# Packed attention and a two-layer network on one core: small-tile products in runs over four PSUM banks, a last chunk of 128 keys, a new order

## Chip, core and metric

The kernel runs on one core of a Trainium2 chip. The metric is the device time of one execution in microseconds (us); several runs are taken and their median counts. The profile is one execution, recorded by the hardware profiler.

## What is computed

For 8 batches of 576 tokens with 8 heads of 64, 32 packed queries a head attend to the keys and values, and the tokens then attend to the 32 packed results. What comes out goes through two layers, 512 to 2048 to 512, with an ELU between them.

```python
def sm_attn(qq, kk, vv):
    s = scale * np.matmul(qq, kk.transpose(0, 1, 3, 2))
    s = s - np.max(s, axis=-1, keepdims=True)
    a = np.exp(s)
    a = a / (np.sum(a, axis=-1, keepdims=True) + 1e-09)
    return np.matmul(a, vv)
p_packed = sm_attn(p, k, v)
out = sm_attn(q, p_packed, p_packed)
...
h = x @ w_in
g = np.where(h > 0.0, h, alpha * (np.exp(np.minimum(h, 0.0)) - 1.0))
return (g @ w_out).astype(np.float32)
```

All arrays are float32, 8 x 8 x 576 x 64 for q, k and v, 8 x 8 x 32 x 64 for p, 512 x 2048 and 2048 x 512 for the weights.

## The kernel before

**Attention of a batch** (`attention`). Heads are taken in 4 pairs (`NPAIR`) of 2 (`G`). `s1` or `s1_half` makes the packed scores of the 576 keys, in two halves of 288: small-tile products whose weights take 64 rows and 32 columns of the array, so that eight of them stand in it side by side. After a softmax over the keys, `tr1` transposes the weights in five chunks of keys, four of 128 and one of 64, and `pv` multiplies them with the values: tiles of 128 rows and 32 columns for four chunks, of 64 rows and 32 columns for the fifth, for each of the two groups. `tr2` transposes the result to `ppT`. `s2` makes the scores of the 576 tokens against the 32 packed results in two halves; their softmax needs many VectorE instructions (`fold`, `smax`, `ssub`, `ssum`, `srec`, `smul`, `unfold`). The attention weights are split into two fp32r parts, `a_hi` and `a_lo`.

**M** (`mstep`, L963). The second attention product and the first layer are folded: `m` is `ppT` times `w_in`, in four chunks of 512 columns a batch, 64-row by 32-column tiles again. ScalarE casts a chunk to `m_hi` (L368, a helper for all copies), VectorE subtracts to `m_lo` (L976). A chunk takes two of the eight PSUM banks until both are done, and for batches 0 and 1 chunks come in halves.

**The two layers.** `h_mm` and `mm` (L1192, L1492) multiply `m` with `a`, three fp32r products for one (hi-hi, lo-hi, hi-lo). ScalarE and VectorE make the ELU (L1204, L1207, L1199; L1501, L1504, L1507) and split the result. Batches 0 and 1 then multiply with `w_out` directly (L1582 to L1585, 512 columns). From batch 2 on, `strassen_pair` takes two blocks of 128 hidden units at a time and makes seven block products in place of eight (L1360, 21 products of 256 columns), with sums of weight blocks from a DRAM buffer (`sw`) and sums of hidden blocks from VectorE (L1284), which are split over 896 columns (L368, L1293). For the pairs in `S_PLAINS` it makes all eight. The sums lie in four PSUM banks (`acc`) for a whole visit of 16 hidden blocks. The 64 tokens over 512 of each batch are kept aside and done with the last batch.

**What sets the order.** `op` records each operation with its due time (`prio`), its engines and cost, the buffers it takes and uses. `schedule` then plays them through with those costs: at each moment the first operation in order of due time runs whose inputs are ready, whose buffers are free and whose engine is idle; a change of kind on TensorE (`mode`) costs `SWITCH`, and within `STAY` of due time another operation of the same kind goes first. What comes out is the order of instructions on each engine, and the due times are tables: `T_ATT1` and `T_ATTS` for the six steps of attention, `TMS` for the four chunks of M, `LI` and `LO` for the conversion of the two weight matrices. PSUM banks are handed out by `Banks.places`. The load of weights and the splitting of `w_in` and `w_out` fill the first 130 us. Until the first layer can start, TensorE runs filling products (`fill`, L191).

Of the kernel before, what the change touches and what calls it, by code (L numbers as in the profile page):

```python
# [12 lines left out]
F32 = mybir.dt.float32  # L13
# [12 lines left out]
def packed_attention_elu_ffn(  # L26
# [29 lines left out]
    G = 2  # L56
# [23 lines left out]
    VISITS = [  # L80
        (0, 0, 0, 8), (0, 1, 0, 8), (1, 1, 0, 8), (0, 1, 8, 12),
        (1, 0, 0, 12), (0, 0, 8, 16), (1, 1, 8, 16), (0, 1, 12, 16),
        (1, 0, 12, 16),
    ]
    T_ATT = [13.5, -16.5, 12.5, 17.5, -18.5, 18.0]
    T_ATT1 = [-33.0, -18.5, -18.0, -4.0, -9.5, -29.0]
    LI = 5.5
    LO = 0.5
    LM = 4.0
    LOOK = 5.75  # L90
    TM = [30.5, 22.5, 36.0, 31.5]
    FIRST = "k v r i1 i0 q".split()
    T_FILL = 1.5
    T_SPARE = 14.0
    AFTER = 1
    T_S2 = -25.5
    STAY = 17
    SWITCH = 0.12
# [5 lines left out]
    S_PLAINS = {  # L104
        (2, 0): [], (2, 1): [0], (3, 0): [0, 7], (3, 1): [], (4, 0): [0], (4, 1): [0, 7],
        (5, 0): [4], (5, 1): [1, 7], (6, 0): [], (6, 1): [1],
    }
    S_VISITS = []
    T_ATTS = {3: [0.0, 2.0, -9.5, -6.0, 10.0, 26.0], 4: [-12.0, -0.5, 15.0, 6.0, 5.5, 22.5], 5: [1.0, 4.5, -9.5, -4.5, 10.5, 24.0], 6: [6.5, 12.5, 6.0, -1.0, 1.0, 23.0], 7: [-2.0, -8.0, 4.5, -5.5, 14.5, 27.0]}
    TMS = {3: [14.5, 29.5, 35.0, 31.0], 4: [21.0, 22.0, 25.0, 36.0], 5: [10.5, 28.5, 36.5, 30.0], 6: [19.5, 12.0, 26.0, 37.5], 7: [17.5, 32.5, 31.0, 30.0]}  # L110
    BY_GROUP = [(0, 0)]
    S1_WHOLE = 3
    T_LC = 1.1
    T_RE = -4.5
    T_RL = 7.0
    T_RX = -1.5
    T_HS = 22.0
    S_FIRST = (2, 0)
    T_SW = 27.5
    T_SL = 13.5  # L120
    T_SE = 6.0
# [14 lines left out]

    class Banks:
# [3 lines left out]
        def places(self, bufs, now):  # L141
            free = [h is None or h.released(now) for h in self.held]
            out = []
            for b in bufs:
                at = [i for i in range(0, len(free), b.n) if all(free[i:i + b.n])]
                if not at:
                    return None

                i = min(at, key=lambda i: (free[i ^ 1], i)) if b.n == 1 else at[-1]
                free[i:i + b.n] = [False] * b.n  # L150
                out.append(i)
            return out
# [4 lines left out]
        def take(self, bufs, now):  # L157
            for b, i in zip(bufs, self.places(bufs, now)):
                b.at = i
                self.held[i:i + b.n] = [b] * b.n  # L160

    class Buf:
        def __init__(self, ring, make, n=1):
            self.ring, self.make, self.n, self.users, self.t = ring, make, n, [], None
            self.free = False
# [27 lines left out]
    def schedule():  # L193
# [18 lines left out]
        seen, live, times = 0, [], sorted(idle_at.values())  # L212
# [9 lines left out]
        def engine_for(o):  # L222
            if o.ready > now or min(idle_at[e] for e in o.on) > now:
                return None
            for r in {id(b.ring): b.ring for b in o.take}.values():
                if not r.grant([b for b in o.take if b.ring is r], now):
                    return None
# [6 lines left out]
        while left:  # L234
            for n, (_, o) in enumerate(live):
# [66 lines left out]
    tmp = ctx.enter_context(tc.tile_pool(name="tmp", bufs=3))  # L302
# [34 lines left out]
    for x in top_ts:  # L337
# [4 lines left out]
        kvq=2, m_hi=NFC, m_lo=NFC, a=2, tmp=3, g=3, e=2, h=2, sw=SW, w8=2, hb=HB,  # L342
        raw=4, top=TOP, ppT=2, pp=1, k0=1, q0=1,
    ).items()}
    R["psum"], R["part"] = Banks(8), Banks(2)
# [18 lines left out]
    def ring_tile(ring, pool, shape, dt, tag, **kw):  # L364
        return Buf(R[ring], lambda: pool.tile(shape, dt, tag=tag, name=tag, **kw))

# [89 lines left out]
    def attention(b, ts):  # L456
# [23 lines left out]
        def temp():  # L480
# [5 lines left out]
            return ring_tile("tmp", tmp, [P, NKC, P], F32, "tmp")  # L486
# [17 lines left out]
        def values(c, h):  # L504
# [4 lines left out]
            return v_b[h // 4].t[:S - 4 * P, o:o + D]  # L509
# [179 lines left out]
        else:  # L689
            kept, o1 = [], None  # L690
            for half in range(2):
                ps = ps1[half]
                o1 = op(
# [16 lines left out]
        for g in range(G):  # L710
# [989 lines left out]
```

## Time and profile before

| | before |
|---|---|
| median of 3 runs | 695.66 us (693.68 to 696.67) |
| span of the profiled execution | 691.8 us |
| TensorE busy | 681.4 us (98%) |
| TensorE, loading weights | 597.3 us (86%) |
| VectorE busy | 586.5 us (85%) |
| ScalarE busy | 437.1 us (63%) |
| granted TensorE clock | 0.999 |

The span runs from the first to the last instruction; the profiled execution has no other time of its own on record, and the runs' median is 3.86 us above its span. Busy time of TensorE is that of its products; weight loads run beside them. A product's duration in the trace is longer than its pace, since the products overlap: the pace is read from one start to the next. A product of float32 operands stands in the trace as two rows and in the order as one; an fp32r product stands as one in both.

### The profile page before, as it was taken

How to read it: one execution, taken by the hardware profiler on the slowest of the kernel's cores; microseconds unless marked ns; L12 is line 12 of the kernel's file. 1: busy time of each engine (PE TensorE's matmuls, PEld its weight loads, DVE VectorE, ACT ScalarE, POOL GpSimd, SP SyncE). 2: the span in 40 equal slices, each digit the busy share in tenths (PEclk: the TensorE clock that was granted, in tenths of full speed). 3: DMA queues.
4: the chain of work that ended last, by engine and by line, in shares of the span. 5: the costliest groups of instructions: out<-in, count | busy, mean ns of one | idle time of the engine just before them, and what ended most of it. 6: DMA issues, size and time to landing. Idle time of an engine off the chain costs nothing. (4 is left out here: it accounts for less than half of the span.)

```text
span 691.8 us, 16246 instructions
## 1 busy us (share of the span) xinstructions
PE 681.4 (98%) x6156; PEld 597.3 (86%) x6156; DVE 586.5 (85%) x1264; ACT 437.1 (63%) x933; POOL 10.7 (2%) x18
## 2 busy tenths in 40 slices
PE   9999999999999999999999999999999999999997
PEld 4567888877789988998989989988899999999997
DVE  4999879998878897859988897669887999978985
ACT  3897987675675666545765656654755568665762
POOL 0000001001120000000000000000000000000000
PEclk9999999999999999999999999999999999999999
DMA  8985756559469877797798787777778868776763
GB/s 345 338 286 193 261 179 166 201 216 309 92 178 270 294 223 255 223 289 258 244 302 283 242 245 221 243 276 267 237 270 267 261 192 271 229 223 199 257 208 126
DMA packets 92366, 166.74 MB, mean 241 GB/s; under 512 B 25728, under 2 KB 26240, under 8 KB 92288
## 3 DMA queue, kind: packets, MB, share of 16 engines
q1 hardware_dynamic: 90560, 162.83, 71.4%
q0 software_dynamic: 1440, 2.62, 2.7%
q8 instruction: 48, 0.79, 0.4%
q14 instruction: 30, 0.25, 0.1%
q10 hardware_dynamic: 288, 0.26, 0.1%
HBM read 141.03 MB, written 24.64 MB: 239 GB/s over the span
## 5 line engine op out<-in xcount | busy, mean ns | idle before, releaser
L1360 PE MATMUL psum<-sw,g 128*128 128x256 f32 x1224 | 182.5, 282 | 0.0
L1360 PEld LDWEIGHTS psum<-sw,g 128*128 128x128 f32 x1224 | 160.9, 189 | 4.9 <-issue 1.7
L368 ACT CAST g<-w 128x896 fp32r<-128x896 f32 (+1 forms) x96 | 87.0, 906 | 89.6 <-DVE w L1284 49.9
L1293 DVE TENSOR_TENSOR g<-w,g 128x896 fp32r<-128x896 f32 (+1 forms) x96 | 100.1, 1043 | 24.0 <-ACT g L368 23.7
L1192 PE MATMUL psum<-a_hi,m_hi 128*128 128x256 f32 (+1 forms) x384 | 115.4, 301 | 0.6 <-DVE w L1199 0.5
L1192 PE MATMUL psum<-a_hi,m_lo 128*128 128x256 f32 (+1 forms) x384 | 113.5, 295 | 0.0
L1192 PE MATMUL psum<-a_lo,m_hi 128*128 128x256 f32 (+1 forms) x384 | 113.5, 295 | 0.0
L1284 DVE TENSOR_TENSOR w<-w 128x128 f32<-128x128 f32 (+1 forms) x258 | 86.0, 333 | 7.2
L1360 PE MATMUL psum<-wo_a,g 128*128 128x256 f32 (+1 forms) x534 | 88.7, 296 | 0.3
L1360 PE MATMUL psum<-wo_b,g 128*128 128x256 f32 (+1 forms) x528 | 85.2, 291 | 0.0
L1192 PEld LDWEIGHTS psum<-a_hi,m_hi 128*128 128x128 f32 x384 | 72.6, 189 | 8.4 <-DVE g L1293 2.1
L1360 PEld LDWEIGHTS psum<-wo_a,g 128*128 128x128 f32 x534 | 74.9, 189 | 5.7 <-issue 0.9
L1360 PEld LDWEIGHTS psum<-wo_b,g 128*128 128x128 f32 x528 | 72.9, 189 | 5.9 <-issue 4.0
L1192 PEld LDWEIGHTS psum<-a_lo,m_hi 128*128 128x128 f32 x384 | 72.6, 189 | 0.3
L1192 PEld LDWEIGHTS psum<-a_hi,m_lo 128*128 128x128 f32 x384 | 72.6, 189 | 0.0
L1204 ACT ACTIVATE e<-psum 128x256 f32<-128x256 f32 x96 | 36.2, 381 | 27.8 <-PE psum L1192 25.1
L1204 ACT ACTIVATE w<-psum 128x512 f32<-128x512 f32 x48 | 28.5, 594 | 35.3 <-PE psum L1192 17.9
L976 DVE TENSOR_TENSOR m_lo<-psum,m_hi 128x1024 fp32r<-128x1024 f32 (+1 forms) x40 | 40.0, 1005 | 3.7 <-ACT m_hi L368 3.5
L1492 PE MATMUL psum<-a_hi,m_hi 128*128 128x256 f32 (+1 forms) x128 | 40.3, 315 | 2.2 <-DVE e L1507 1.8
L1199 DVE SCALAR_TENSOR_TENSOR w<-e,psum 128x256 f32<-128x256 f32 x96 | 38.6, 414 | 2.3 <-ACT e L1207 2.1
L368 ACT CAST m_hi<-psum 128x1024 fp32r<-128x1024 f32 (+1 forms) x40 | 33.6, 845 | 10.9 <-PE psum L963 10.7
L1207 ACT ACTIVATE e<-e 128x256 f32<-128x256 f32 x96 | 39.7, 418 | 1.1
(127 smaller groups left out, 1161.6 us busy)
## 6 DMA issues: line engine op xcount, KB each, us to landing
sw<-sw_dram SPq DMA_DIRECT2D x344, 256.0 KB, 3.9
kvq<-in_v SPq DMA_DIRECT2D x16, 640.0 KB, 5.6
raw<-in_w_in SPq DMA_DIRECT2D x16, 512.0 KB, 5.5
raw<-in_w_out SPq DMA_DIRECT2D x16, 512.0 KB, 5.0
sw_dram<-sw SPq DMA_DIRECT2D x32, 256.0 KB, 2.5
kvq<-in_qT SPq DMA_DIRECT2D x14, 576.0 KB, 5.8
out<-part SPq DMA_DIRECT2D x30, 256.0 KB, 3.3
kvq<-in_kT SPq DMA_DIRECT2D x7, 640.0 KB, 5.8
```

The lines of the kernel that those rows point to most:

```text
L368: (nc.scalar.copy if e == "ACT" else nc.vector.tensor_copy)(out=out, in_=in_)
L976: nc.vector.tensor_tensor(out=m_b[1].t[:, :, fs], in0=ps.t[:, :, :w], in1=m_b[0].t[:, :, fs].bitcast(F32), op=ALU.subtract,)
L1192: nc.tensor.matmul(ps, lhsT=m_b[p].t[:, g, o:o + P], rhs=st.a.t[q][:, g, cols], start=(n == 0), stop=(n == 3 * G - 1),)
L1199: nc.vector.scalar_tensor_tensor(out=out, in0=e_, scalar=-1.0, in1=ps, op0=ALU.add, op1=ALU.max)
L1204: nc.scalar.activation(out=out, in_=ps, func=AF.Relu, scale=-1.0)
L1207: nc.scalar.activation(out=x, in_=x, func=AF.Exp, scale=-1.0)
L1284: nc.vector.tensor_tensor(out=out, in0=x, in1=y, op=o)
L1293: nc.vector.tensor_tensor(out=g_b.all[:, 7 * P:(7 + b1 - b0) * P], in0=blocks(b0, b1), in1=g_b.all[:, :(b1 - b0) * P].bitcast(F32), op=ALU ...
L1360: nc.tensor.matmul(a.t[:, at * H:at * H + rhs.shape[-1]], lhsT=operand(blk, p), rhs=rhs, start=new and n == k == 0, stop=a.final == (u, mi ...
L1492: nc.tensor.matmul(ps_b.t[:, :n_tok], lhsT=m_b[x].t[:, g, o:o + P], rhs=st.a.t[y][:, g, cols], start=(n == 0), stop=(n == 3 * G - 1),)
```

## The change

**Four banks for a run of small tiles.** `mstep` can make two chunks of M in one operation (`n=2`) that takes four banks; `M_BOTH` names seven places. `S1_BOTH` (batches 5 and 7) and `S2_BOTH` (batch 2) do the same with the two halves of the scores. `PV_WHOLE` makes `pv` of both groups one operation in five batches. Batch 2's key scores (`S1_WHOLE` 3 to 2) go from whole to halves. In `schedule`, an operation that needs more than two banks and finds too few free is kept, and no other TensorE operation that takes banks goes ahead of it. Sums come in pairs of banks (`bank_pair`).

**128 keys in the last chunk.** `tr1` takes the last 128 of the 576 keys as its fifth chunk, and the array of values carries zeros for the 64 of these that the fourth chunk has already. All of `pv` then has tiles of 128 rows.

**Buffers and order.** The three temporaries are handed out as they come free (`Slots`), not in turn. All tables of due times are new; the visits 6 and 7 of the list are exchanged; `S_PLAINS` has 14 pairs in place of 10. An unused branch for plain products (`H_PLAIN`) leaves `mstep`.

```diff
-    T_ATT1 = [-33.0, -18.5, -18.0, -4.0, -9.5, -29.0]
-    LI = 5.5
-    LO = 0.5
+    T_ATT1 = [-33.0, -98.5, -101.0, -91.0, -7.0, -102.0]
+    LI = 13.5
+    LO = -1.5
...
-    STAY = 17
-    SWITCH = 0.12
+    STAY = 35.0
+    SWITCH = 0.145
...
-        (2, 0): [], (2, 1): [0], (3, 0): [0, 7], (3, 1): [], (4, 0): [0], (4, 1): [0, 7],
-        (5, 0): [4], (5, 1): [1, 7], (6, 0): [], (6, 1): [1],
+    S_PLAINS = {(2, 0): [], (2, 1): [], (3, 0): [0, 4, 7], (3, 1): [], (4, 0): [6], (4, 1): [0, 1, 2, 3, 7], (5, 0): [1, 2], (5, 1): [1, 7], (6, 0): [], (6, 1): [1]}
...
-    S1_WHOLE = 3
+    S1_WHOLE = 2
+    S1_BOTH = [5, 7]
+    S2_BOTH = [2]
+    PV_WHOLE = [1, 4, 5, 6, 7]
+    M_BOTH = [(2, 2), (3, 0), (4, 0), (4, 2), (5, 0), (6, 0), (7, 0)]
...
+    class Slots:
+        def __init__(self, n):
+            self.held = [None] * n
+        def free(self, now):
+            return [i for i, h in enumerate(self.held) if h is None or h.released(now)]
+        def grant(self, bufs, now):
+            return len(self.free(now)) >= len(bufs)
...
         def engine_for(o):
-            if o.ready > now or min(idle_at[e] for e in o.on) > now:
+            nonlocal kept
+            if o.ready > now:
                 return None
-            for r in {id(b.ring): b.ring for b in o.take}.values():
-                if not r.grant([b for b in o.take if b.ring is r], now):
-                    return None
+            if kept and "PE" in o.on and o is not kept and any(b.ring is R["psum"] for b in o.take):
+                return None
+            rings = {id(b.ring): b.ring for b in o.take}.values()
+            short = [r for r in rings if not r.grant([b for b in o.take if b.ring is r], now)]
+            if short == [R["psum"]] and sum(b.n for b in o.take if b.ring is R["psum"]) > 2:
+                kept = kept or o
+            if short or min(idle_at[e] for e in o.on) > now:
+                return None
...
+    def bank_pair():
+        x = [banks(1) for _ in range(2)]
+        x[0].mate, x[1].mate = x[::-1]
+        return x
...
+            if b in S1_BOTH:
+                o1 = op(
+                    t, {"PE": 0.97}, lambda e: [s1_half(e, half, ps1[half]) for half in range(2)], ld_k,
+                    take=ps1 + e1s, use=k_b, after=[free], mode=1,
+                )
...
             def tr1(e, g=g, e1=e1, pt=pt):
                 for c in range(NKC):
-                    n = min(P, S - c * P)
+                    k0 = min(c * P, S - P)
                     nc.tensor.transpose(
-                        out=pt.t[:n, c // 4, (c % 4) * P:(c % 4 + 1) * P],
-                        in_=flat(e1)[:, c * P:c * P + n], identity=ident,
+                        out=pt.t[:, c // 4, (c % 4) * P:(c % 4 + 1) * P],
+                        in_=flat(e1)[:, k0:k0 + P], identity=ident,
                     )
...
+        if b in PV_WHOLE:
+            o = op(
+                ts[2], {"PE": 1.16}, lambda e: [pv(e, g) for g in range(G)], ld_v + tr_done,
+                take=[ps_v], use=v_b + e1T, mode=2,
+            )
...
-    def mstep(b, c, part, parts_, prio, deps=()):
+    def mstep(b, c0, part, parts_, prio, n=1):
...
-        ps = banks(2)
+        pss = [banks(2) for _ in cs]
...
+            for c, ps in zip(cs, pss):
+                for pair in range(NPAIR):
+                    for g in range(G):
+                        nc.tensor.matmul(
...
+                if (b, c) in M_BOTH:
+                    mstep(b, c, 0, 1, prio, 2)
+                elif (b, c - 1) not in M_BOTH:
+                    mstep(b, c, 0, 1, prio)
...
-            accs[mine] = [banks(1) for _ in range(3)] + [accs["rest"][3] if both else banks(1)]
+            if both:
+                accs[mine] = [banks(1) for _ in range(3)] + [accs["rest"][3]]
+            else:
+                accs[mine] = bank_pair() + bank_pair()
...
-            out[:, n, :S - 512, 2 * E:] = x[:, 512:, n * E // 2:(n + 1) * E // 2]
+            out[:, n, 640 - S:, 2 * E:] = x[:, 512:, n * E // 2:(n + 1) * E // 2]
```

What becomes of the order at three places. TensorE at the key scores of batch 4 before, two halves of 8 small products (L601) apart, with first-layer (L1192) and output products (L1360) between:

```order
L1192 MATMUL psum<-a_hi,m_lo 128x320
L601 MATMUL psum<-kvq 32x288 x8
L1192 MATMUL psum<-a_hi,m_hi 128x320
L1192 MATMUL psum<-a_lo,m_hi 128x320
L1192 MATMUL psum<-a_hi,m_lo 128x320
L1192 MATMUL psum<-a_hi,m_hi 128x320
L1192 MATMUL psum<-a_lo,m_hi 128x320
L1192 MATMUL psum<-a_hi,m_lo 128x320
L1360 MATMUL psum<-sw,g 128x256 x6
L601 MATMUL psum<-kvq 32x288 x8
L1360 MATMUL psum<-wo_a,g 128x256 x6
```

The same place after; the lines are numbered anew, L601 is now L635, L1192 is L1240, L1360 is L1411:

```order
L1240 MATMUL psum<-a_hi,m_lo 128x320
L1411 MATMUL psum<-wo_b,g 128x256 x6
L1411 MATMUL psum<-sw,g 128x256 x3
L635 MATMUL psum<-kvq 32x288 x16
L1411 MATMUL psum<-wo_b,g 128x256 x3
L1411 MATMUL psum<-sw,g 128x256 x9
L1411 MATMUL psum<-wo_b,g 128x256 x6
```

The two halves stand in one row of 16. TensorE at batch 3's M before, one of its lone chunks (L963):

```order
L1192 MATMUL psum<-a_hi,m_lo 128x320
L1360 MATMUL psum<-wo_b,g 128x256 x3
L1360 MATMUL psum<-sw,g 128x256 x3
L963 MATMUL psum<-w_in_sb,ppT 32x512 x8
L1360 MATMUL psum<-sw,g 128x256 x6
L1360 MATMUL psum<-wo_b,g 128x256 x6
L1360 MATMUL psum<-sw,g 128x256 x3
```

And at batch 3's chunks 0 and 1 after (L1013):

```order
L1411 MATMUL psum<-wo_b,g 128x256 x3
L1411 MATMUL psum<-sw,g 128x256 x3
L1013 MATMUL psum<-w_in_sb,ppT 32x512 x16
L1411 MATMUL psum<-sw,g 128x256 x6
L1411 MATMUL psum<-wo_b,g 128x256 x6
L1411 MATMUL psum<-sw,g 128x256 x3
L1411 MATMUL psum<-wo_b,g 128x256 x3
L1411 MATMUL psum<-sw,g 128x256 x3
L1240 MATMUL psum<-a_hi,m_hi 128x320
L1240 MATMUL psum<-a_lo,m_hi 128x320
```

Two chunks stand in one row of 16, with 21 output products behind them and then the first layer. VectorE at that place after, where it takes the chunks' subtraction (L1031) behind a split (L1341) and ahead of the next ELU (L1247):

```order
L1332 TENSOR_TENSOR w_3633<-w_3633 128x128
L1341 TENSOR_TENSOR g<-w_3633,g 128x896
L1031 TENSOR_TENSOR m_lo<-psum,m_hi 128x1024 x2
L402 COPY hb<-psum 128x64 x2
L1247 SCALAR_TENSOR_TENSOR w_3757<-e,psum 128x256 x2
L1341 TENSOR_TENSOR g<-w_3757,g 128x512
L402 COPY hb<-psum 128x64 x2
L1247 SCALAR_TENSOR_TENSOR w_3804<-e,psum 128x256 x2
```

Both subtractions stand together, ahead of the ELU of the next first-layer products. Counted over the whole program, TensorE has 57 runs of small-tile products between large ones before and 43 after, transposes alone not counted.

## Rows read from the trace of the kernel before

**Rows 1.** Busy us by stretch: start:end length, PE, PEld, DVE, ACT, POOL, clock, DMA

```profile
130.00:600.00 470.00, 468.84 (x4372) 418.96 (x4356) 400.28 (x864) 286.54 (x598) 7.12 (x8) 1.00 0.78 246
600.00:691.80 91.80, 86.90 (x724) 86.69 (x722) 74.52 (x149) 51.70 (x86) 0.00 (x0) 1.00 0.63 204
sum 691.80, PE 681.36 PEld 597.29 DVE 586.50 ACT 437.05 POOL 10.65; mean PE 97.34 PEld 85.33 DVE 83.79 ACT 62.44 POOL 1.52
```

**Rows 2.** Waits of TensorE: who waited for whom, us in total, times, longest

```profile
PE psum L1492 <- DVE e L1507: 1.8, 3, 1.1
```

**Rows 3.** Timeline of TensorE, output pairs: start us, us, line, shapes, count

```profile
247.02 0.52 PE L1360 MATMUL psum<-wo_a,g 128*128 128x256 f32 x3
...
249.53 0.30 PE L1192 MATMUL psum<-a_hi,m_hi 128*128 128x320 f32 x1
...
283.00 3.00 PE L1360 MATMUL psum<-wo_a,g 128*128 128x512 f32 x12
285.83 0.30 PE L1192 MATMUL psum<-a_hi,m_hi 128*128 128x320 f32 x1
```

**Rows 4.** Timeline of TensorE around a lone chunk of M

```profile
262.57 0.51 PE L1360 MATMUL psum<-sw,g 128*128 128x256 f32 x3
263.01 1.09 PE L963 MATMUL psum<-w_in_sb,ppT 64*32 64x512 f32 x16
264.03 0.98 PE L1360 MATMUL psum<-sw,g 128*128 128x256 f32 x6
264.85 0.87 PE L1360 MATMUL psum<-wo_b,g 128*128 128x256 f32 x6
```

**Rows 5.** Timeline of TensorE around two chunks of M in a row

```profile
565.22 0.52 PE L1360 MATMUL psum<-sw,g 128*128 128x256 f32 x3
565.67 1.95 PE L963 MATMUL psum<-w_in_sb,ppT 64*32 64x512 f32 x32
567.55 0.62 PE L1360 MATMUL psum<-wo_b,g 128*128 128x256 f32 x3
568.01 0.52 PE L1360 MATMUL psum<-sw,g 128*128 128x256 f32 x3
```

**Rows 6.** Timeline of TensorE around a lone half of the token scores

```profile
212.46 0.52 PE L1360 MATMUL psum<-sw,g 128*128 128x256 f32 x3
212.91 0.71 PE L788 MATMUL psum<-kvq,ppT 64*32 64x288 f32 x16
213.56 0.39 PE L1192 MATMUL psum<-a_hi,m_hi 128*128 128x256 f32 x1
213.78 0.28 PE L1192 MATMUL psum<-a_lo,m_hi 128*128 128x256 f32 x1
```

**Rows 7.** Timeline of TensorE around two halves of the token scores in a row

```profile
164.97 0.63 PE L1585 MATMUL psum<-wo_b,g 128*128 128x512 f32 x2
165.53 1.20 PE L788 MATMUL psum<-kvq,ppT 64*32 64x288 f32 x32
166.66 0.39 PE L1492 MATMUL psum<-a_hi,m_hi 128*128 128x256 f32 x1
166.88 0.28 PE L1492 MATMUL psum<-a_lo,m_hi 128*128 128x256 f32 x1
```

**Rows 8.** Timeline of TensorE inside one values product, in four narrow windows

```profile
198.86 0.65 PE L742 MATMUL psum<-kvq,tmp 128*32 128x64 f32 x32
...
199.28 0.42 PE L742 MATMUL psum<-kvq,tmp 128*32 128x64 f32 x7
...
199.44 0.32 PE L742 MATMUL psum<-kvq,tmp 64*32 64x64 f32 x8
...
199.69 0.65 PE L742 MATMUL psum<-kvq,tmp 128*32 128x64 f32 x32
```

**Rows 9.** Timeline of ScalarE and VectorE, emptying the chunk of rows 4

```profile
264.75 1.01 ACT L368 CAST m_hi<-psum 128x1024 fp32r<-128x1024 f32 x1
...
265.79 1.22 DVE L976 TENSOR_TENSOR m_lo<-psum,m_hi 128x1024 fp32r<-128x1024 f32 x1 [0.33 <-ACT m_hi L368]
```

More of the change, by code (lines that the diff above doesn't have):

```diff
@@ L135, in take @@
             self.taken += bufs
+    class Slots:
[5 more added lines that the diff above has]
+            return len(self.free(now)) >= len(bufs)
+        def take(self, bufs, now):
+            for b, i in zip(bufs, self.free(now)):
+                b.at, self.held[i] = i, b
     class Banks:
@@ L210, in schedule @@
         conv = set(conv_ops)
-        seen, live, times = 0, [], sorted(idle_at.values())
+        seen, live, times, kept = 0, [], sorted(idle_at.values()), None
         def look():
@@ L234, in schedule @@
         while left:
+            kept = None
             for n, (_, o) in enumerate(live):
@@ L726, in tr1b @@
             def tr1b(e, pt=pt, eT=eT):
[L727 to L728 removed]
+                copy(e, eT.t[:, 4, :], pt.t[:, 1, :P])
             t = ts[1]
@@ L779, in attention @@
         prev = []
+        s2_ps, s2_ts, s2_op = [banks(2) for _ in range(2)], [temp() for _ in range(4)], None
         for half in range(2):
-            ps = banks(2)
-            t1, t2 = temp(), st.af if whole else temp()
+            ps = s2_ps[half]
+            t1, t2 = s2_ts[2 * half], st.af if whole else s2_ts[2 * half + 1]
             mx, sm = {}, {}
@@ L956, in mstep @@
         w = FC // parts_
         fs = slice(part * w, (part + 1) * w)
-        ps = banks(2)
+        pss = [banks(2) for _ in cs]
         def mm(e):
-            for pair in range(NPAIR):
-                for g in range(G):
-                    nc.tensor.matmul(
-                        ps.t[cols_of(pair), g, :w], lhsT=st.ppT.t[rows_of(g), pair, :],
-                        rhs=w_in_sb[rows_of(g), pair, c * FC + part * w:c * FC + (part + 1) * w],
-                        start=True, stop=True,
-                    )
@@ L969, in mstep @@
-        whole = b in H_PLAIN and c == 0
-        def hi(e):
-            out = m_b[0].t[:, :, fs]
-            copy(e, out.bitcast(F32) if whole else out, ps.t[:, :, :w])
-        def lo(e):
-            nc.vector.tensor_tensor(
-                out=m_b[1].t[:, :, fs], in0=ps.t[:, :, :w], in1=m_b[0].t[:, :, fs].bitcast(F32),
-                op=ALU.subtract,
-            )
-        fl = [c * 4 + part * 4 // parts_ + n for n in range(4 // parts_)]
-        pre = [w_ready[True, f] for f in fl] + [st.ppT_op] + list(deps)
@@ L1561, in packed_attention_elu_ffn @@
         if first:
-            acc = [banks(1) for _ in range(n_t)]
+            acc = bank_pair()
         def out_mm(e, one=slice(0, 1), i=i, f=f, g_b=g_b, acc=acc, first=first, final=final, g_whole=g_whole):
```

143 lines of the change are left out of this document (80 added, 63 removed).

## The prediction, made before the changed kernel was run

> **What bounds the kernel now.** I read the busy time by stage first [rows 1]: over the whole span of 691.8 us TensorE is busy for 681.4, VectorE for 586.5 and ScalarE for 437.1. TensorE lacks 10.4 us in all; 4.90 of them are the tail behind its last product, 1.16 lie between 130 and 600 us, and so 4.4 before 130 us. Then TensorE's waits [rows 2]: the longest sum is 1.8 us in three waits for VectorE's ELU instruction, the longest of them 1.1. So TensorE's own stream sets the end: what shortens or lengthens it moves the end one for one, and a saving on VectorE or ScalarE counts only where TensorE waits for it. The pace of the large products: 21 of 256 columns from 247.02 to 249.53 take 2.51 us, 0.1195 each [rows 3]. With it I price a visit of small-tile products: the stretch from a large product ahead of it to one behind it, less the large products in that stretch.
>
> **A visit has a fixed price.** A lone chunk of the M product (8 fp32 products in the order, 16 in the trace) stands at 263.01. From 262.57 to 264.85 are 2.28 us with 3+6 large products, 1.08 us: the visit costs 1.20 [rows 4]. Two chunks in a row stand at 565.67: from 565.22 to 568.01 are 2.79 us with 6 large products, 0.72: 2.07 [rows 5]. Twice 1.20 less 2.07 is 0.33 us, which belongs to the coming and going, and the second chunk itself adds 0.87. The query scores agree. A lone half at 212.91: from 212.46 to 213.78 are 1.32 us with 3+1 large products, 0.48: 0.84 [rows 6]. Two halves at 165.53: from 164.97 to 166.88 are 1.91 us with two products of 512 columns (0.236 each, below) and one of 256: 1.32 [rows 7]. Twice 0.84 less 1.32 is 0.36. I take 0.34.
>
> **Term 1, fewer visits.** Counted in TensorE's order, the stretches of small-tile products between large ones (transposes alone not counted) go from 57 to 43: the key scores of batches 3 to 7 come in one run each, where two halves stood apart; the M chunks mostly as pairs; the query halves of batches 1 and 3 to 7 in one run each. All 14 lie behind the first layer's first product, where large products stand ready for the place: 14 x 0.34 = **-4.8 us**, between -4.6 and -5.0 by the two prices.
>
> **Term 2, the last chunk of keys.** In the packed values product the fifth chunk of 64 keys uses tiles of 64 rows between those of 128. In one batch the 128-row part runs from 198.86 to 199.44 (0.58), the 64-row part to 199.69 (0.25), and then the same once more [rows 8]. The last of eight rounds begins at 199.28, so a round takes 0.42/7 = 0.06; from there to 199.44 are 0.16, 0.10 more than a round; and the 64-row part's two rounds take 0.25 in place of 0.12, 0.13 more. So each change of the tile's height inside the product costs about 0.12. With 128 keys there is none. Three changes go in each of six batches and two in batch 7, where an M product now stands ahead in the same run; batch 0's stand where TensorE only fills time. 20 x 0.12 = **-2.4 us**, between -2.0 and -2.6. The chunk's own rounds stay. The fifth transposition takes 128 columns of keys instead of 64; at worst that is half a product's pace, 0.06, in each of 14, +0.8; I take 0, since its moving side has 128 columns either way. The wider copy behind it works on the same columns in more partitions, and lies in the time that VectorE and ScalarE have over [rows 1].
>
> **Term 3, more plain pairs.** The table of pairs without the seven-product scheme goes from 10 entries to 14: two more with 12 products of 512 columns, two more with 6 of 512 and 12 of 256. A seven-product pair is 2.51 us; the 12 products at 283.00 are followed at 285.83, so 2.83, or 0.236 each [rows 3]; 6 x 0.236 + 12 x 0.1195 is 2.85. Four times 0.32 to 0.34: **+1.3 us**. VectorE loses four rounds of sums and SyncE 16 weight loads; neither sets the end, so I credit nothing.
>
> **Term 4, the new order.** The due times change throughout: batch 1's values, transposes and second query half are asked for as early as may be, the later batches' attention mostly earlier, the conversion of the first layer's weights earlier and of the second's later. What stands on TensorE ahead of its first layer product, and in the tail, reads nearly the same before and after. In between, waits may go or come. From below, the 4.4 us before 130 us less the start shrink: about 3 us gained. From above stand rivals 1 and 2. The chains are of the same kinds and laid out by the same planner, so I take 0. The planner also keeps other bank users off TensorE while an operation waits for four banks; in the program that is only an order, priced with rival 1.
>
> The sum: -4.8 - 2.4 + 1.3 = -5.9 us, a span of 691.8 - 5.9 = 685.9. The runs' median of 695.66 is 3.86 above the profiled span; with that kept, **689.8 us**, 0.85% less.
>
> **Rival 1: four banks starve the first layer (slower).** In a visit to the second layer by seven products four of the eight banks hold sums. A merged M takes the other four, and no first-layer product starts until ScalarE has cast and VectorE subtracted a chunk. The lone chunk that starts at 263.01 gets its cast at 264.75 (1.01 us) and its subtraction at 265.79 (1.22), so its banks come free at 267.01, 4.0 us after its start [rows 4, 9]. In the new order, at the place shown, 21 output products, 2.5 us, stand behind the merged M's 2.0, then a first-layer product: 4.5 us for the first chunk, which is enough by 0.5 if ScalarE comes no later than here; the second chunk's subtraction ends 1.2 later, and a second first-layer product follows about 0.9 behind the first. Nine more operations than before take four banks at once (seven M, batch 5's and 7's key scores and batch 2's query scores, less batch 2's key scores). It decides from 5.9/9 = 0.66 us a place; at the longest wait seen, 1.1 us [rows 2], it is +9.9: 699.7, slower by 0.6%. Against it: the runs of rows 5 and 7 filled four banks in a row and nothing waited behind them, and output products do stand there. The Trainium skill, "TensorEngine Tiling (Array Packing)", section "PSUM Bottleneck", speaks for it: tiling speeds TensorE up but not the emptying of PSUM, which may become the bottleneck. The trace agrees as to the ratio, 1.01 and 1.22 us of emptying for a chunk that adds 0.87; by that rule 699.7 would be the likeliest time.
>
> **Rival 2: the early stage waits longer.** Before 130 us VectorE converts weights, does batch 1's softmax and the ELUs that free banks, and there lie 4.4 us of the 10.4 that TensorE lacks [rows 1]. If the new order doubles what of it is not the start, +3: 692.8, within 0.5%. For it: the due times of batch 1 move most. Against: the conversions' order there changes by a few places only.
>
> **Rival 3: the merged runs wait inside.** The order says two halves in a row, but the second waits for its banks or its load with TensorE standing, and the 0.34 comes back as a wait. Then the change doesn't do what it says, term 1 is nothing, and 695.66 - 2.4 + 1.3 = 694.6, within 0.5%. Against it: rows 5 and 7 show no wait inside.
>
> **How the numbers follow.** Forecast 0.64 (686.5 to 692.2); rival 1 0.12, of which 0.08 is slower and the rest a mild form that keeps half the gain; rival 2 0.14; rival 3 0.10. 0.5%, about what a measurement of this kernel can tell from no change, is 692.2 and 699.1. Faster: the forecast and 0.12 from the milder ends of the rivals, 0.76; slower 0.08; same 0.16. The range, 686.2 to 695.0, takes in rivals 2 and 3 and term 4's gain, and leaves out the strong form of rival 1 and a tenth on the fast side.
>
> **What would show it.** Term 1: the M product in rows of 32 that cost near 2.07 by the same subtraction, score runs of 32 near 1.32. Term 2: the values product in one shape, its large successor about 1.3 us behind its start, where it is 1.66 now (two of 0.58 and 0.25). Term 3: 132 products of 512 columns in the second layer's pairs at 0.236. Term 4: TensorE lacking 10 us again. It would be wrong if TensorE waits for ScalarE or VectorE right behind the merged products (rival 1), if the lack before 130 us doubles (rival 2), or if small-tile runs hold waits (rival 3).

## The result and the profile after

The changed kernel takes 686.99 us (686.48 to 687.5, four runs) where the kernel before takes 694.67 in the same comparison: a ratio of 0.989, 95% interval 0.9863 to 0.9917. The profiled execution has a span of 684.7 us, 7.1 less than before; 5.9 less were forecast.

| | before | after |
|---|---|---|
| span of the profiled execution | 691.8 us | 684.7 us |
| TensorE busy | 681.4 | 673.6 |
| TensorE idle | 10.4 | 11.1 |
| VectorE busy | 586.5 | 577.7 |
| ScalarE busy | 437.1 | 439.3 |

TensorE has less to do, by 7.8 us, and lacks slightly more. First the busy time by stage behind 130 us (columns as in rows 1), then TensorE's waits (as in rows 2):

```profile
130.00:600.00 470.00, 468.04 (x4350) 423.53 (x4349) 393.82 (x843) 288.97 (x610) 7.01 (x8) 1.00 0.75 238
600.00:684.70 84.70, 79.81 (x668) 79.61 (x667) 68.25 (x134) 48.04 (x77) 0.00 (x0) 0.99 0.63 202
```

```profile
PE psum L757 <- ACT tmp L662: 1.1, 1, 1.1
...
PE psum L757 <- DVE g L402: 0.5, 1, 0.5
...
PE psum L757 <- DVE m_lo L1031: 0.4, 1, 0.4
...
PE psum L1543 <- DVE e L1558: 0.2, 1, 0.2
```

The wait that led the list before, 1.8 us for VectorE's ELU [rows 2], is down to 0.2. New ones stand at `tr1` (L757), which before had one of 0.3; the lack between 130 and 600 us went from 1.16 [rows 1] to 1.96. What the visits cost, in three timelines of TensorE (start, us, line, shapes, count): two chunks of M, two halves of the token scores, one values product, each between large products.

```profile
247.04 0.52 PE L1411 MATMUL psum<-sw,g 128*128 128x256 f32 x3
247.49 1.95 PE L1013 MATMUL psum<-w_in_sb,ppT 64*32 64x512 f32 x32
249.37 0.62 PE L1411 MATMUL psum<-wo_a,g 128*128 128x256 f32 x3
249.82 1.24 PE L1411 MATMUL psum<-sw,g 128*128 128x256 f32 x9
```

```profile
297.20 1.09 PE L1411 MATMUL psum<-wo_b,g 128*128 128x512 f32 x4
298.25 1.20 PE L831 MATMUL psum<-kvq,ppT 64*32 64x288 f32 x32
299.38 1.20 PE L1411 MATMUL psum<-wo_b,g 128*128 128x512 f32 x4
```

```profile
239.76 0.87 PE L1411 MATMUL psum<-wo_a,g 128*128 128x256 f32 x6
240.56 1.32 PE L779 MATMUL psum<-kvq,tmp 128*32 128x64 f32 x80
241.81 0.41 PE L1240 MATMUL psum<-a_hi,m_hi 128*128 128x320 f32 x1
```

M: 249.82 - 247.04 is 2.78, less six products at 0.1195: 2.06, as in rows 5. The two halves: 299.38 - 297.20 less four products at 0.236 is 1.24, and the product after the next comes 0.10 late: 1.34, for 1.32 in rows 7. The values product is one shape now, and its successor starts 1.25 us behind its start, where it was 1.66.

I then went through the starts of all TensorE rows, priced every visit by the row of its kind that has no wait, and every large product by its pace. By kind: the values products at 1.45 each (before 1.85), 2.7 us less for the 20 changes of height; 14 visits fewer, 4.8 less; the large products 1.1 more. That is -6.4. The rest, -0.7, is waits, and a difference of two large items: those inside and at visits went from 1.4 to 5.3 us, those in front of large products from 5.0 to 0.4. Of the 1.4, 0.37 is a load at 308 us that none of five other runs of the old order waited for. Start and tail are the same.

### The profile page after: what moved, and what is told of

The parts are those of the page before. It is cut to its first block, busy times and chain, and to the rows that moved or that the text cites. A ratio compares the mean times of both kernels' runs of the same rounds, so it can differ in the third digit from the quotient of the medians.

```text
span 684.7 us, 16158 instructions
## 1 busy us (share of the span) xinstructions
PE 673.6 (98%) x6127; PEld 597.4 (87%) x6133; DVE 577.7 (84%) x1242; ACT 439.3 (64%) x947; POOL 10.6 (2%) x18
## 4 chain that ended last, share of the span: by engine, by line
PE 86%; DVE 5%; ACT 4%; DMA 3%; issue 1%; SPq 0%; DVEq 0%; ACTq 0%
PE psum L1411 41%; PE psum L1240 22%; PE psum L1543 5%; PE psum L1013 3%; PE psum L1633 3%; PE psum L1634 3%; PE psum L1636 3%; DMA raw<-in_w_in 2%; PE psum L779 1%; PE psum L757 1%; PE psum L831 1%; PE psum L208 1%; PE psum L635 1%; ACT top L402 1%; DVE sw L1163 1%
## 5 line engine op out<-in xcount | busy, mean ns | idle before, releaser
L1411 PE MATMUL psum<-sw,g 128*128 128x256 f32 x1176 | 175.6, 282 | 0.0
L1411 PEld LDWEIGHTS psum<-sw,g 128*128 128x128 f32 x1176 | 155.4, 189 | 2.5 <-issue 2.5
L402 ACT CAST g<-w 128x896 fp32r<-128x896 f32 (+1 forms) x96 | 85.4, 891 | 59.9 <-DVE w L1332 33.1
L1341 DVE TENSOR_TENSOR g<-w,g 128x896 fp32r<-128x896 f32 (+1 forms) x96 | 98.3, 1025 | 22.5 <-ACT g L402 21.7
L1240 PE MATMUL psum<-a_hi,m_hi 128*128 128x256 f32 (+1 forms) x384 | 114.6, 299 | 0.3
L1240 PE MATMUL psum<-a_hi,m_lo 128*128 128x256 f32 (+1 forms) x384 | 113.5, 296 | 0.0
L1240 PE MATMUL psum<-a_lo,m_hi 128*128 128x256 f32 (+1 forms) x384 | 113.4, 295 | 0.0
L1411 PE MATMUL psum<-wo_a,g 128*128 128x256 f32 (+1 forms) x555 | 93.3, 300 | 0.1
L1332 DVE TENSOR_TENSOR w<-w 128x128 f32<-128x128 f32 (+1 forms) x246 | 82.1, 334 | 6.8
L1411 PE MATMUL psum<-wo_b,g 128*128 128x256 f32 (+1 forms) x531 | 86.9, 293 | 0.0
L1411 PEld LDWEIGHTS psum<-wo_a,g 128*128 128x128 f32 x555 | 78.4, 189 | 5.2 <-issue 1.7
L1411 PEld LDWEIGHTS psum<-wo_b,g 128*128 128x128 f32 x531 | 73.3, 189 | 6.2 <-issue 3.5
L1240 PEld LDWEIGHTS psum<-a_hi,m_hi 128*128 128x128 f32 x384 | 72.7, 189 | 5.3 <-ACT e L1255 1.4
L1240 PEld LDWEIGHTS psum<-a_lo,m_hi 128*128 128x128 f32 x384 | 72.6, 189 | 0.5
L1240 PEld LDWEIGHTS psum<-a_hi,m_lo 128*128 128x128 f32 x384 | 72.6, 189 | 0.0
L1031 DVE TENSOR_TENSOR m_lo<-psum,m_hi 128x1024 fp32r<-128x1024 f32 (+1 forms) x40 | 39.6, 1006 | 8.4 <-ACT m_hi L402 8.3
L1247 DVE SCALAR_TENSOR_TENSOR w<-w,psum 128x512 f32<-128x512 f32 x48 | 32.5, 679 | 11.8 <-ACT w L1255 11.8
L1247 DVE SCALAR_TENSOR_TENSOR w<-e,psum 128x256 f32<-128x256 f32 x96 | 38.4, 413 | 2.7 <-ACT e L1255 2.3
```

The costliest lines, as they stand in the source:

```text
L402: (nc.scalar.copy if e == "ACT" else nc.vector.tensor_copy)(out=out, in_=in_)
L1031: nc.vector.tensor_tensor(out=m_b[1].t[:, :, fs], in0=ps.t[:, :, :w], in1=m_b[0].t[:, :, fs].bitcast(F32), op=ALU.subtract,)
L1240: nc.tensor.matmul(ps, lhsT=m_b[p].t[:, g, o:o + P], rhs=st.a.t[q][:, g, cols], start=(n == 0), stop=(n == 3 * G - 1),)
L1247: nc.vector.scalar_tensor_tensor(out=out, in0=e_, scalar=-1.0, in1=ps, op0=ALU.add, op1=ALU.max)
L1332: nc.vector.tensor_tensor(out=out, in0=x, in1=y, op=o)
L1341: nc.vector.tensor_tensor(out=g_b.all[:, 7 * P:(7 + b1 - b0) * P], in0=blocks(b0, b1), in1=g_b.all[:, :(b1 - b0) * P].bitcast(F32), op=ALU ...
```

## Experiments

Two facts on how they are read. In kernels with the same TensorE order I compared the start of the same product. In the repeats of both kernels such products keep their distance behind 130 us to 0.1 us but for three places (0.42 at 308 us in the old order, 0.25 at 432 and 0.14 at 642 in the new one), so that a step of 0.3 us can be seen at its place; ahead of 130 us they differ by chance (below). `b_joined`, `a_uncovered`, `b_again` and `b_elu_again` are one execution each, and only their traces are read. And `defer(n, k)`, written for these runs, takes the n-th operation of an engine, with what hangs on it, out of the finished order and puts it behind the next k operations of that engine.

**The last chunk alone** (`b_keys128`): on the kernel before, only

```diff
-                n = min(P, S - c * P)
...
-                        ps_v.t[cols_of(pair), g, :D], lhsT=e1T[g].t[:n, c, cols_of(pair)],
+                        ps_v.t[cols_of(pair), g, :D], lhsT=e1T[g].t[:, c, cols_of(pair)],
```

with the same in `tr1`, its copy and the array of values.

> The kernel before with the last chunk of keys at 128 and nothing else of the change; its order is as before. My theory (term 2): every values product costs less by three changes of the tile's height. The changed kernel's values products cost 1.45 us each as a visit where the kernel before has 1.85 or 1.86, so 7 x 0.4 = 2.8 us less: a span of 689.0 (691.8 before), ratio 0.996. The forecast's own price, 20 x 0.12, gives 689.4. A rival: the cheaper values product in the changed kernel comes from its new place or from both groups standing in one operation; then the visits stay at 1.85 here and the span at 691.8. A second rival: the fifth transposition, now 128 columns of keys, costs 0.06 more each, 0.8 in all, and the span is 689.8.

Ratio 0.9963 (0.9945 to 0.9981), about 2.6 us; span 687.0. Of the span's 4.8, 2.2 lie ahead of 130 us: 0.4 for batch 1's values product, the rest chance. Behind it the distance grows by 0.41 to 0.43 at each of five values products and by 0.2 at the one that shares its run with M (0.36 more is a wait for a load at 308 that is not met). The timeline at the place of rows 8:

```profile
196.20 1.32 PE L740 MATMUL psum<-kvq,tmp 128*32 128x64 f32 x80
197.45 0.50 PE L1580 MATMUL psum<-wo_b,g 128*128 128x512 f32 x1
```

The price belongs to the height of the tiles: 0.41 for three changes is 0.137 each, where I had 0.12; the two of batch 7 cost 0.1 each. Five transposes cost 0.55 as before, so the second rival falls too.

**Runs of M cut again** (`a_split_m`): on the changed kernel

```diff
+            if e == "PE" and held:
+                held.second(e)
+                held = None
+            if getattr(o, "second", None):
+                held = o
```

> The changed kernel with its seven merged M operations cut again: the first chunk stands where the run stood, the second behind the next operation of TensorE; the rest of the order is the same. That makes seven visits more. My theory (term 1, a fixed price of 0.34 us a visit): the two chunks cost 1.21 each where the run costs 2.07, so 7 x 0.34 = +2.4 us on the changed kernel's span of 684.7: 687.1. A rival: the gain of the runs lies in the order made around them, not in the visits; then the span stays within 0.5 of 684.7. A second rival (four banks starve the first layer): cut in two, the first chunk's banks come free as before and the second's later, waits go or come, and the span moves by more than 3 us either way.

Ratio to before 0.9939 (0.9918 to 0.9961); span 688.0. Behind 130 us TensorE loses 2.6 in all. At six of the seven places it loses 0.34 to 0.36; one of them, with the large products ahead and behind:

```profile
263.79 0.51 PE L1413 MATMUL psum<-sw,g 128*128 128x256 f32 x3
264.23 1.09 PE L1013 MATMUL psum<-w_in_sb,ppT 64*32 64x512 f32 x16
265.25 0.98 PE L1413 MATMUL psum<-sw,g 128*128 128x256 f32 x6
266.16 1.09 PE L1013 MATMUL psum<-w_in_sb,ppT 64*32 64x512 f32 x16
267.18 0.97 PE L1413 MATMUL psum<-wo_b,g 128*128 128x256 f32 x6
267.99 0.28 PE L1413 MATMUL psum<-sw,g 128*128 128x256 f32 x1
```

From 263.79 to 267.99 are 4.20 us with 15 large products, 1.79: 2.41 for two visits, 1.21 each, where the run costs 2.06. At the seventh place, 194 us, the cut makes no visit: the second chunk lands behind a half of the token scores in the same run of small tiles. The 0.32 lost there is a wait, of that half's weight loads for VectorE:

```profile
196.29 0.15 PEld L831 LDWEIGHTS psum<-kvq,ppT 64*32 64x32 f32 x11 [0.23 <-DVE tmp L839]
```

So the cut adds six visits and not seven, and they cost 2.1 together. At these six places the order is the same but for the cut, so the gain of a run is the visit's price, as term 1 says. The Trainium skill, "TensorEngine Tiling (Array Packing)", section "Key Properties", says that a change of the tiling mode drains the engine; the trace agrees in so far as a visit costs 0.34 us beyond its products.

**Runs without the banks** (`b_joined`): on the kernel before

```diff
+        for n, k in [(357, 3), (248, 2)]:
+            defer(n, k)
```

> The kernel before with two pairs of key score halves put in one run in TensorE's order, batches 4 and 5, and nothing else: no other banks, no other due times. In batch 4 both halves use the same two banks; in batch 5 an M chunk behind the second half uses the first half's banks. My theory (the fixed price of a visit, and rival 3's wait inside): a bank pair is emptied 2.4 us after its half starts (0.8 to the first copy, then copy, maximum and copy in turn), so the second half in batch 4 waits 1.9 and the M chunk in batch 5 1.4, less 0.34 for each visit saved: +1.6 and +1.1 at these places, a span 2.7 longer than before but for chance ahead of 130 us. The other theory: joining alone gives 0.34 a place, since the emptying runs beside it; then TensorE is 0.7 earlier behind both places.

```profile
258.08 0.72 PE L602 MATMUL psum<-kvq 64*32 64x288 f32 x16
260.14 1.01 PE L602 MATMUL psum<-kvq 64*32 64x288 f32 x16 [1.35 <-ACT tmp L369]
```

TensorE loses 1.56 us at batch 4 and 0.98 at batch 5, as worked out ahead (1.6 and 1.1); the other theory's 0.34 gained did not come. This is rival 3 as it looks when the banks are missing: the run needs four of its own, and what the change does in the planner is the condition for term 1.

**The work behind a merged run** (`a_uncovered`): on the changed kernel `defer(264, 4)`, the run of batch 3 behind the 21 output products shown ahead of the prediction.

> The changed kernel with one piece of TensorE's order turned round: the two chunks of M of batch 3 that stand at 263.27 us, ahead of 21 output products, are moved behind them, so that first-layer products follow directly. It tells what the work behind a merged run is worth (rival 1 of the prediction). By the rows of the kernel before a chunk's two banks come free 4.0 us after it starts; the run itself lasts 2.07; so TensorE should stand for about 1.9 us in front of the first-layer product behind it, for VectorE's subtraction, and the span should be longer by 1.5 to 2.0 than the changed kernel's 684.7. The other theory: the emptying of four banks is hidden by itself, since other banks are free at that place; then no wait over 0.3 us stands there and the span is the same.

First the changed kernel at that place (PE, ACT and DVE rows), then the run:

```profile
263.27 1.95 PE L1013 MATMUL psum<-w_in_sb,ppT 64*32 64x512 f32 x32
...
264.48 1.92 ACT L402 CAST m_hi<-psum 128x1024 fp32r<-128x1024 f32 x2
...
265.62 2.35 DVE L1031 TENSOR_TENSOR m_lo<-psum,m_hi 128x1024 fp32r<-128x1024 f32 x2
...
267.72 0.31 PE L1240 MATMUL psum<-a_hi,m_hi 128*128 128x320 f32 x1
```

```profile
265.47 1.95 PE L1014 MATMUL psum<-w_in_sb,ppT 64*32 64x512 f32 x32
266.66 1.93 ACT L403 CAST m_hi<-psum 128x1024 fp32r<-128x1024 f32 x2 [2.35 <-PE psum L1014]
267.71 2.36 DVE L1032 TENSOR_TENSOR m_lo<-psum,m_hi 128x1024 fp32r<-128x1024 f32 x2 [2.27 <-ACT m_hi L403]
268.99 0.42 PE L1241 MATMUL psum<-a_hi,m_hi 128*128 128x320 f32 x1 [1.57 <-DVE m_lo L1032]
```

Every product behind the place stands 1.6 us later; span 686.1. So the work behind a merged run is worth that much here. But the run does not show that the banks are what TensorE lacks: these are batch 3's first first-layer products, and the chunk is their input as well as the holder of their first bank. The first two read only `m_hi`, whose first half is cast by about 267.6 (half of 1.93 behind 266.66), and still they stand until the first subtraction ends at 268.9: that is the bank. The third reads `m_lo`, which the same subtraction makes. A free bank would have let the first two go ahead, 0.29 us by their pace; that is my estimate of the banks' own part, and no run separates the two. In the changed kernel the first chunk's subtraction is done by about 266.8 (half of 2.35 behind 265.62) and bank and input are asked for at 267.72: about 0.9 to spare, where I had 0.5.

**Waiting operations moved back** (`a_moved`): on the changed kernel

```diff
+        for n, k in [(436, 2), (433, 2), (165, 2), (163, 1), (160, 1), (112, 1), (72, 1)]:
+            defer(n, k)
```

> The changed kernel with five stretches of TensorE's order moved behind the one or two large operations that follow them, where its trace shows TensorE standing for an input or a bank: the transposes at 129.75, 180.94 and 407.95 us (0.71, 0.62 and 1.36 us more than such a visit costs elsewhere), the key scores at 85.27 (0.78 more) and the second chunk of M at 175.38 (0.73 more). All else is in the same order. My theory: these 4.2 us are waits inside visits that the new order itself made; moved, they go, less 0.34 each for the two that leave a run: -3.5 us, a span of 681.2. A rival: the wait is set by VectorE's and ScalarE's work as a whole and only shows up elsewhere on TensorE; then the span stays within 0.7 of 684.7, and what these visits lose appears in front of later products.

Slower than the changed kernel by 6.1 in the span (690.8); ratio to before 0.9967 (0.9954 to 0.998). TensorE is 2.4 behind at 129 us already, 1.5 of it at 36 us, ahead of all that is moved; the rest comes at and behind the moved operations. Neither theory. TensorE's waits:

```profile
PE psum L1412 <- DVE m_lo L1032: 1.6, 1, 1.6
...
PE psum L1634 <- DVE mx L645: 1.5, 1, 1.5
```

The output products that the transposes and the chunk were moved behind (L1412, L1634) wait as well: they take banks for their sums that VectorE has yet to empty of M and of key scores. I read it so that in the changed kernel one wait covered the next, and that moving an operation uncovered it.

**What the transposes wait for** (`a_keep_first`). The chain behind 407.95, in the changed kernel (ScalarE's copies, VectorE's maxima, then the exponential):

```profile
402.23 0.40 ACT L402 COPY tmp<-psum 128x288 f32<-128x288 f32 x1 [2.61 <-PE psum L635]
402.66 0.76 DVE L644 TENSOR_REDUCE mx<-psum 128x2 f32<-128x576 f32 x1 [0.17 <-ACT tmp L402]
403.45 0.70 ACT L402 COPY tmp<-psum 128x288 f32<-128x288 f32 x2 [0.82 <-DVE mx L644]
404.19 0.76 DVE L644 TENSOR_REDUCE mx<-psum 128x2 f32<-128x576 f32 x1 [0.77 <-ACT tmp L402]
...
407.02 0.78 ACT L662 ACTIVATE tmp<-tmp,nb 128x576 f32<-128x576 f32 x1
...
407.95 0.77 PE L757 MATMUL psum<-ident,tmp 128*128 128x128 f32 x5 [1.06 <-ACT tmp L662]
```

Both engines only read these banks, and yet they take turns: the program makes one wait for the other. The Trainium skill, "PSUM — Partial Sum Buffer", section "PSUM bank collisions raise a hardware error", asks for that, for two readers too; the rows agree that the turns are taken, and no run here shows what would happen without. The edit on the changed kernel takes each half's two copies ahead of its maximum:

```diff
+                o.first = kept[-G:]
...
+        for x in [x for x, _ in plan if getattr(x, "first", None)]:
+            for y in x.first:
...
+                if at > to:
+                    plan.insert(to, plan.pop(at))
```

> The changed kernel with another order between two engines at the key scores of batches 2 to 7: ScalarE's two copies of a half go ahead of VectorE's maximum over the same half, where copy, maximum and copy took turns. In the changed kernel's trace they take turns over the two halves at 402.23 (0.40, 0.76, 0.70 for two, 0.76, 0.40: 3.2 us), which the planner takes for work side by side. With the copies first, the maximum of one half runs beside the copies of the other: 0.8 + 0.76 + 0.76 = 2.3 us. My theory: the exponential and with it the transposes' inputs come 0.7 to 0.9 us earlier, and TensorE's waits at the transposes behind two halves in a row, 1.36 us at 407.95 and perhaps 0.62 at 180.94, shrink by about that: a span of 683.3 to 684.0. A rival: the transposes wait for M's emptying, which stands on the same two engines, and the span is the same within 0.5.

```profile
402.10 1.31 ACT L402 COPY tmp<-psum 128x288 f32<-128x288 f32 x4 [2.61 <-PE psum L635]
402.83 1.42 DVE L644 TENSOR_REDUCE mx<-psum 128x2 f32<-128x576 f32 x2 [0.47 <-ACT tmp L402]
```

The four copies stand together and the two maxima run beside them, 2.15 us in place of 3.2 (2.3 foreseen), and the wait at the transposes is gone there. But the ratio to before is 0.9896 (0.9873 to 0.9919), the changed kernel's, and the span 684.6. At other batches first-layer products now wait for the maximum, 1.06 us between 455 and 465; behind 119 us gains and losses leave 1.1 gained, and this execution had come to 119 us 1.0 late. Hence the same for three batches (`a_keep_some`):

```diff
-                o.first = kept[-G:]
+                o.first = kept[-G:] if b in (2, 3, 6) else None
```

> The changed kernel with ScalarE's copies of the key scores ahead of VectorE's maximum in batches 2, 3 and 6 alone. With this order in all of batches 2 to 7 the same products of TensorE stood earlier by 0.46 us at 130, by 0.85 at 183 and by 1.34 at 409, and later by 0.2 at 250, by 0.3 at 403 and by 1.06 between 455 and 465, where first-layer products then wait for VectorE's maximum. My theory: each of these belongs to its batch, so the three kept ones give -0.46 - 0.85 - 1.04 = -2.3 us on the changed kernel's 684.7 to 685.2: a span near 682.6, ratio about 0.986. A rival: the gains are given back behind by other waits wherever they are made; then the span is 684.5 to 685 and the ratio stays 0.989 to 0.990.

684.39 us, ratio to before 0.9867 (0.9839 to 0.9895), span 682.7: 2.0 less than the changed kernel's first trace, 2.5 less than its second. Product by product the three places give 0.5, 0.85 and 1.0 as foreseen; 1.1 is lost at 247, where VectorE stood 1.44 us for a store of leftovers and M's second chunk for VectorE; and the wait at 85 us is missing, as in the changed kernel's repeat (below), which gives 0.7. So the span meets the 682.6 expected partly by luck: behind 119 us the edit brought 1.3 and not 2.3. It is the fastest of all these kernels; in the ratios its interval still overlaps the changed kernel's.

**The early stage** (`b_elu_first`): on the kernel before, VectorE's order by `defer`,

```diff
+        for n, k in [(97, 1), (116, 1), (115, 1), (162, 1), (209, 1), (213, 2)]:
+            defer(n, k)
```

> The kernel before with six VectorE instructions moved by one or two places, so that at five places between 55 and 120 us the ELU instruction that frees a bank goes first: ahead of a transpose and a conversion at 55.99 and 66.17, of a conversion at 94.06, of sums of weights at 115.73 and 118.25. TensorE's order is untouched. There its first-layer products stand 0.66, 1.40, 0.39, 0.34 and 0.26 us behind their pace. My theory: these waits of the early stage come from VectorE's order alone, and what the new order gained there is of this kind; most of the 3.0 us go, the span falls by 2.0 to 2.8 from 691.8 to about 689.4, ratio 0.9965. A rival: VectorE's work is the bound in this stage, so that what one ELU gains the next one loses; then the sum of such waits stays within 1 us of before, and the span too.

Ratio 1.0009 (0.9995 to 1.0024): nothing gained. In the trace the waits of 0.66 and 1.40 are gone, but TensorE came to 25 us 2.3 late. Hence three repeats, of this kernel, of the kernel before and of the changed one, none with an edit of its own:

> Once more the kernel before with the ELU instructions first at five places. In its first trace TensorE stood 2.3 us behind the kernel before at 25 us, ahead of all that is moved, and 0.2 behind at 120: 2.1 us made good, but the timed runs show nothing gained. If the moved ELUs are worth 2 us by themselves, TensorE is about 2 us ahead of the kernel before at 130 us in a run that starts as it does. If the stage ends by something else (loads and conversions), TensorE gets to 130 us within 0.7 us of the kernel before again, whatever its start.

> The kernel before once more, nothing altered. In its first trace 3.0 us of waits for VectorE's ELU stand between 55 and 120 us, and 4.4 us of idle TensorE before 130. If they belong to the order they come back at the same first-layer products with the same sizes. If they are chance of the loads and of the start, they differ: two other kernels with the same order of TensorE in that stage had the product that stands at 119.85 here at 117.62 and 120.02. Behind 130 us every product should keep its distance to 0.1 us.

> The changed kernel once more, nothing altered. It tells how far the waits of one profiled execution repeat. If the waits found in the first trace belong to the order, this one has them at the same places: 1.36, 0.71 and 0.62 us at three transposes, 0.78 and 0.73 inside two runs of small tiles, and less than 1 us in front of first-layer products between 40 and 120 us, where the kernel before has 3.0; the span is 684.7 within 1. If they are chance, places and sizes change, and the span moves by several us.

Busy time ahead of 130 us, of before, its repeat, `b_elu_first`, its repeat, the changed kernel and its repeat in this order:

```profile
0.00:130.00 130.00, 125.63 (x1078) 91.64 (x1086) 111.71 (x254) 98.81 (x250) 3.53 (x10) 1.00 0.72 250
```

```profile
0.00:130.00 130.00, 125.30 (x1062) 91.49 (x1062) 111.49 (x253) 98.70 (x250) 3.53 (x10) 1.00 0.72 249
```

```profile
0.00:130.00 130.00, 125.71 (x1061) 91.61 (x1062) 110.69 (x253) 97.99 (x250) 3.53 (x10) 1.00 0.71 248
```

```profile
0.00:130.00 130.00, 124.13 (x1045) 89.94 (x1046) 108.30 (x245) 96.74 (x247) 3.54 (x10) 0.99 0.70 243
```

```profile
0.00:130.00 130.00, 125.74 (x1113) 94.29 (x1120) 115.66 (x268) 102.28 (x262) 3.62 (x10) 1.00 0.74 259
```

```profile
0.00:130.00 130.00, 126.92 (x1119) 93.97 (x1120) 115.52 (x267) 101.89 (x262) 3.53 (x10) 1.00 0.74 258
```

The kernel before repeats its ELU waits at the same products (0.67 and 1.24 for 0.66 and 1.40, and larger ones at 95 and 99) and its span to 0.1 us (691.9). With the ELUs first, both runs reach 130 us later than before, by 0.6 and 3.2. In both, ScalarE stood longer in the first 50 us for the weights' loads, and VectorE's conversions behind it: 3.4 and 3.2 us against 2.0 in both traces of the kernel before. The second run:

```profile
34.80 0.78 ACT L369 CAST top<-raw 128x512 f16<-128x512 bf16 x1 [2.06 <-DMA raw<-in_w_out]
35.62 0.69 DVE L405 SCALAR_TENSOR_TENSOR raw<-raw,top 128x512 uint32<-128x512 uint32 x1 [1.32 <-ACT top L369]
```

So waits there can be moved without a gain, and loads have a part in where the stage ends; how large a part, and whether the edit itself has a hand in the late loads, stays open. The changed kernel's repeat has the later waits at the same places and sizes (1.37, 0.71, 0.63 and 0.73), but 0.78 at 85 us not, and a span of 685.2. In front of large products ahead of 130 us, waits come to 4.3 and 4.5 us in the two traces of the old order and to 0.8 and 1.3 in those of the new, so their going belongs to the order. But by the rows above TensorE lacks 4.4 and 4.7 us in all before 130 in the old order and 4.3 and 3.1 in the new: between 0.1 and 1.6 us less, which two traces each don't tell from chance.

**Ten plain pairs** (`a_plains10`): the changed kernel with the table `S_PLAINS` of before.

> The changed kernel with the table of plain pairs of the kernel before (10 pairs in place of 14); the planner lays the rest out anew. My theory (term 3): each plain pair costs TensorE 0.32 to 0.34 us more than a seven-product pair, so four fewer give -1.3 us if nothing waits: a span of 683.4 by pace alone. A rival: the four plain pairs were worth it, since each saves VectorE a round of sums and split (three sums of 0.36, a split of 1.09) and SyncE four weight loads; then TensorE waits for VectorE or for the loads in the second layer's stage in place of the 1.3, and the span is 684.7 or more. The waits in front of the second layer's products tell which.

706.86 us, ratio to before 1.0179 (1.0149 to 1.0209), span 704.3. That doesn't tell the theories apart: with four pairs fewer, in five entries of the table, the planner made another order, in which TensorE stands for a whole softmax of the tokens:

```profile
434.15 0.61 PE L1243 MATMUL psum<-a_hi,m_hi 128*128 128x320 f32 x1 [7.92 <-ACT tmp L405]
```

What a plain pair saves VectorE and the loads was not measured.

## Why the prediction was right, and where it was off

- **The bound**: right. TensorE's busy time fell by 7.8 and the span by 7.1, with VectorE 8.8 us less busy; giving VectorE or ScalarE another order moved the end only where TensorE waited for it.
- **Term 1** (-4.8): right in price and number. The cut shows it for six visits, 2.1 us where 6 x 0.34 is 2.0; the other eight rest on the same price read from rows.
- **Term 2** (-2.4): the right mechanism, mis-sized. It measures -2.7: 0.137 a change and not 0.12.
- **Term 3** (+1.3): 1.1 by pace, 0.231 for a product of 512 columns. Whether VectorE's relief is worth anything is open.
- **Term 4** (0): the net was near that, -0.7, well inside what I gave it, but not because waits neither came nor went. 4.6 us of waits in front of large products went and 3.9 came at the visits. I had rated it by the sum of idle time; 10.4 and 11.1 us hide that exchange.
- **Rival 1** (four banks starve TensorE) did not come. Behind none of the merged M does a first-layer product wait over 0.3 us, since output products stand there that need no new bank; take them away and 1.57 us appear, for a bank and for an input that the rival had not named; both come with the same subtraction. By the rule of the Trainium skill, "TensorEngine Tiling (Array Packing)", section "PSUM Bottleneck" (tiling speeds TensorE up and not the emptying of PSUM), 699.7 would have been likeliest. The 686.99 measured speak against it here. Waits came elsewhere: where key scores and M follow each other in one run, a chunk waits 0.73 inside and the transposes behind wait 0.6 and 1.4, 2.7 of the 3.9. None of these operations takes four banks at once (`M_BOTH` and `S1_BOTH` do not name them), and `a_keep_first` took the two waits of the transposes away with the banks as they were: these belong to the turns of ScalarE and VectorE.
- **Rival 2** did not come: the lack before 130 us is 4.3 and 3.1 where it was 4.4 and 4.7. **Rival 3** came at two places, 0.78 and the 0.73 just named (the first of them not in the repeat), not at the merged runs.

The forecast was short by 1.2 us in the span: 0.3 from term 2, 0.2 from term 3 and 0.7 from term 4, which is no more than the early stage varies by from run to run. The median came out 2.8 below the 689.8 forecast, 0.8 us inside the fast end of the range. The other 1.6 are the step from the span to the median: I carried 3.86 over, and here it is 2.3. In the changed kernel's four runs each time stands 1.8 above its span, so the profiled execution before took about 693.6 by my estimate, 2.1 less than the median that I compared it with; that was chance, and no term of the sum.

## What to carry to other kernels

Price a switch of tile shape from lone and paired visits in the trace, and look for work that can share a visit; then ask which banks the run needs and what TensorE can do while they are emptied, since joining without banks costs more than the visit. A wait that ends just before another one is no gain until both are gone: look up what the next instruction in line waits for before moving the first. And a table of due times fits the rest of its tables: change one entry, and look at the whole order anew.

## What the runs showed of the hardware

In the run with ten plain pairs TensorE's granted clock fell (columns as in rows 1; the seventh is the clock):

```profile
418.00:427.00 9.00, 5.03 (x65) 1.35 (x64) 7.96 (x14) 1.72 (x3) 0.00 (x0) 0.72 0.55 166
427.00:434.50 7.50, 0.35 (x1) 0.29 (x1) 6.50 (x12) 2.21 (x6) 0.00 (x0) 0.50 0.50 175
434.50:440.00 5.50, 4.76 (x16) 4.11 (x16) 2.98 (x10) 3.12 (x9) 0.00 (x0) 0.50 0.05 12
```

It stood at 1.00 up to 418, was 0.50 while TensorE stood for 7.92 us, which is the level of 1.2 GHz, and still 0.50 for the products behind it: those of 320 columns go at 0.267 us each, where 0.147 is their pace at 1.00. The price of a visit has a part behind it that I had not looked for: the second large product starts 0.08 to 0.10 us late, after visits as after longer waits.
